# Retention steps of 128 tokens split into two halves of 64, every product in a 64x64 quarter of the matmul array

## The chip, the cores and the metric

One core of a Trainium2 chip runs the whole program. The metric is the device time of one execution in microseconds (us), as the median of three runs. The engines that matter here are TensorE (PE in the profile, its weight loads PEld), VectorE (DVE), ScalarE (ACT), GpSimd (POOL, used here for one scaling and a few transfers) and SyncE (SP, whose queue issues nearly all the DMAs).

## What is computed

A retention layer (linear attention with a decay for each head) is followed by two pairs of dense layers. The retention, cut to what matters:

```
gamma = 1 - 2 ** (-5 - arange(H))
for t in range(S):
    state = gamma * state + k[t] outer v[t]          # for each batch and head, 64 x 64
    y[t]  = scale * q[t] @ state
```

with 4 batches, 8 heads, 768 tokens and head size 64. Its output, 3072 tokens of 512 channels, goes through `x @ w_in`, `h - tanh(h)`, `@ w_out` (512 to 2048 to 512) and then through a second such pair with an ELU between. Weights come as 64-bit arrays and are converted in the kernel; the dense products are made as three fp32r products each of high and low parts.

## The kernel before

Tokens are taken in six blocks of 512: 128 tokens of each of the four batches. A retention step `s` (0 to 23 in the code, so the change's steps 5 to 24 are `s` = 4 to 23) treats one batch's 128 tokens of one block, and the four steps of block b run while the first dense layer works on block b - 1. `s // 4` is the block, `s % 4` the batch. Steps 0 to 3 have functions of their own (`scores0`, `out0`, `state0`), since no state comes before them.

A step has two places in TensorE's order. `ret_scores` puts eight fp32 matmuls there (`scores_mm`, L350: contraction over the 64 rows of a head, 128 keys by 128 queries), then VectorE multiplies both halves by the decay mask `dtab` into `pt` (L315) and scales q in place by `qtab` (L357). One dense group pair later `ret_out` puts `out_mm` there: eight matmuls of state by q (L374, 64 rows, 64 columns, 128 queries), eight of `pt` by v (L380, 128 rows, 64 columns, 128 queries), and `state_mm`, eight of k by v (L388, 128 rows, 64 columns, 64 wide). After it ScalarE and VectorE write the high and low part of the result to the dense layer's input `x` (L306, L309), and VectorE multiplies the state by gamma to the 128th (L584) and adds the new part (L312). In the last block (`s` = 20 to 23) no state is made.

An fp32 matmul leaves two records of MATMUL and two of LDWEIGHTS in the trace, so eight matmuls stand as sixteen.

The dense first layer takes 12 matmuls of 512 columns for a slice of `h` (`first_std`) and 12 for the four `acc` tiles (`second`), all at L410, alternating through the order list `order0`; `events` says after which `h` group a step's scores and its out come. Loads for a step are requested two or three groups ahead (`loads`). A planner (`Plan`) fixes, before the program runs, the order on every engine and the place of every tile from estimated durations and due times; tiles of class A (4 KB a partition) share 37 places, of class B 16, PSUM has 8. TensorE's own order is the one in which the code calls `op("PE", ...)`, and each engine runs its order strictly.

During the first quarter of steps (`s` = 4 to 7) the weights of the first layer are still being loaded and converted, by ScalarE (L326, L306) and VectorE (L330, L334, L309).

Of the kernel before, what the change touches and what calls it, by code (L numbers as in the profile page):

```python
# [264 lines left out]
def retention_moe_kernel(ctx: ExitStack, tc: tile.TileContext, dims, ins, out):  # L265
# [10 lines left out]
    NQ = NF // 2  # L276
    assert H * D == DM and 2 * D == P and B == SPB and NB == NCH and S % P == 0 and NB % 2 == 0
# [6 lines left out]
    qtab = const.tile([P, NP, P], F32, name="qtab")  # L284
    dtab = const.tile([P, 2, NP, P], F32, name="dtab")
    ktab = const.tile([P, H, 1], F32, name="ktab")
    gtab = const.tile([P, NP, 1], F32, name="gtab")
# [56 lines left out]
    def half(p, j):  # L344
        j = (j + p) % 2
        return slice(j * D, (j + 1) * D)

    def scores_mm(sc, qk):
# [6 lines left out]
    def scale_q_(qk):  # L355
        q = qk[:, 0, :].rearrange("p (a i) -> p a i", a=NP)
        nc.vector.tensor_tensor(out=q, in0=q, in1=qtab, op=ALU.mult)  # L357

    def scale_k_(kn):
        k = kn.rearrange("p (h d) -> p h d", h=H)  # L360
        nc.gpsimd.tensor_tensor(out=k, in0=k, in1=ktab.to_broadcast([P, H, D]), op=ALU.mult)

    def out_first_mm(o, v, pt):
        for p, j, r in pairs():
            h = 2 * p + j
            nc.tensor.matmul(
                out=o[half(p, j), p, :], lhsT=v[:, h * D:(h + 1) * D], rhs=pt[:, j, p, :],
                start=True, stop=True, skip_group_check=True,
            )

    def out_mm(even, odd, stc, qk, v, pt):
        outs = [(even, odd)[p % 2][:, p // 2, :] for p in range(NP)]
        for p, j, r in pairs():
            nc.tensor.matmul(  # L374
                out=outs[p][half(p, j)], lhsT=stc[r, p, :], rhs=qk[r, 0, p * P:(p + 1) * P],
                start=(p < 2), stop=False, skip_group_check=True,
            )
        for p, j, r in pairs():
            h = 2 * p + j
            nc.tensor.matmul(  # L380
                out=outs[p][half(p, j)], lhsT=v[:, h * D:(h + 1) * D], rhs=pt[:, j, p, :],
                start=False, stop=True, skip_group_check=True,
            )

    def state_mm(ds, v, kn):
# [7 lines left out]
    def state_view(odd):  # L393
        return odd[:, NP // 2:, :].rearrange("p a (b d) -> p (a b) d", d=D)

    def load_qk(t, s):
        nc.sync.dma_start(out=t, in_=ins["qkv"][s][:, 0:2, :])

# [16 lines left out]
    with tc.manual_schedule():  # L415
# [15 lines left out]
        nc.scalar.dma_start(out=dtab, in_=ins["dtab"])  # L431
        nc.scalar.dma_start(out=ktab, in_=ins["ktab"])
        nc.scalar.dma_start(out=gtab, in_=ins["gtab"])
# [3 lines left out]
        taken = {"m0", "b4"}  # L437
# [3 lines left out]
            {"raw": 12, "g": 4, "gl": 8, "qk": 2, "pt": 1, "pt0": 2, "w1r": 5, "T": 1, "wop": 4, "w2r": 8, "r3": 1,  # L441
             "v": 4, "kn": 4, "w32": 4, "ev": 4, "raw2": 2, "r": 5},
# [11 lines left out]
        QK, V, KN, PT, ST = {}, {}, {}, {}, {}  # L454
# [82 lines left out]
        def ret_load(s, rel):  # L537
            if s not in QK:
                t = QK[s] = Buf("A", [P, 2, TB], F32, f"qk{s}", "qk")
                dma(lambda: load_qk(t.ap, s), 4096, w=[t], rel=rel)  # L540
            if s not in V:
                t2 = V[s] = Buf("B", [P, TB], F32, f"v{s}", "v")
                dma(lambda: load_v(t2.ap, s), 2048, w=[t2], rel=rel)
            if s // B == NCH - 1:
                return
            if s not in KN:
                t3 = KN[s] = Buf("B", [P, TB], F32, f"kn{s}", "kn")
                dma(lambda: load_kn(t3.ap, s), 2048, w=[t3], rel=rel)
            k = KN[s]
            op("POOL", 1.2, lambda: scale_k_(k.ap), w=[k], name=f"scalek{s}")  # L550

        def ret_scores(s):
            q = QK[s]
            c = [Buf("P", [P, NP, P], F32, f"sc{s}_{j}") for j in range(2)]
            op("PE", 1.55, lambda: scores_mm([x.ap for x in c], q.ap), r=[q], w=c, lat=0.2, name=f"scores{s}")
            p = PT[s] = Buf("A", [P, 2, NP, P], F32, f"pt{s}", "pt")
            for j in range(2):
                op("DVE", DVE5, lambda j=j: mul(p.ap[:, j], c[j].ap, dtab[:, j]), r=[c[j]], w=[(p, j)], name=f"mask{s}")
            op("DVE", DVE5, lambda: scale_q_(q.ap), r=[qtab_b], w=[q], name=f"scaleq{s}")

        def ret_out(s):
            b, c = divmod(s, B)
            q, vv, p, sv = QK.pop(s), V.pop(s), PT.pop(s), ST[c // 2]
            even = Buf("P", [P, NP // 2, P], F32, f"oe{s}")
            odd = Buf("P", [P, NP, P], F32, f"oo{s}")
            op("PE", 1.8, lambda: out_mm(even.ap, odd.ap, sv.ap[:, c % 2], q.ap, vv.ap, p.ap),
               r=[q, vv, p, (sv, c % 2)], w=[even, (odd, 0)], lat=0.2, name=f"out{s}")
            last = b == NCH - 1
            if not last:
                k = KN.pop(s)  # L570
                op("PE", 0.6, lambda: state_mm(state_view(odd.ap), vv.ap, k.ap), r=[k, vv], w=[(odd, 1)], lat=0.2, name=f"state{s}")
            if c == 0:
                x_tile(b)
            x = X[b]
            sl = slice(c * P, (c + 1) * P)
            for i, (ks, o) in enumerate(((slice(0, NP, 2), even), (slice(1, NP, 2), odd))):
                def view(o=o, i=i):
                    return o.ap if i == 0 else o.ap[:, 0:NP // 2, :]

                op("ACT", 0.32, lambda ks=ks, view=view: copy(x.ap[:, 0, ks, sl], view()), r=[o], w=[(x, (0, c, i))], due=3.0, name=f"xhi{s}")  # L580
                op("DVE", 0.36, lambda ks=ks, view=view: sub(x.ap[:, 1, ks, sl], view(), x.ap[:, 0, ks, sl].bitcast(F32)),
                   r=[o, (x, (0, c, i))], w=[(x, (1, c, i))], due=4.0, name=f"xlo{s}")
            if not last:
# [144 lines left out]
        qtab_b = Buf("D")  # L728
# [7 lines left out]

        def load0_kn(s):
            t = KN[s] = Buf("B", [P, TB], F32, f"kn{s}", "kn")
            dma(lambda: load_kn(t.ap, s), 2048, w=[t], name=f"kn{s}")
            op("POOL", 1.2, lambda: scale_k_(t.ap), w=[t], name=f"scalek{s}")  # L740

        def scores0(s):
            c = [Buf("P", [P, NP, P], F32, f"sc{s}_{j}") for j in range(2)]
            op("PE", 1.15, lambda: scores_mm([x.ap for x in c], stage.ap[:, s]), r=[(stage, s)], w=c, lat=0.2, name=f"scores{s}")
            p = PT[s] = Buf("A", [P, 2, NP, P], F32, f"pt{s}", "pt0")
            for j in range(2):
                op("DVE", DVE5, lambda j=j: mul(p.ap[:, j], c[j].ap, dtab[:, j]), r=[c[j]], w=[(p, j)], name=f"mask{s}")
# [13 lines left out]
        def state0(j):  # L761
            ds = Buf("P", [P, 2, NP, D], F32, f"dsp{j}")
            for c in range(2):
                vv, k = V.pop(2 * j + c), KN.pop(2 * j + c)
                op("PE", 0.7, lambda c=c, vv=vv, k=k: state_mm(ds.ap[:, c], vv.ap, k.ap), r=[vv, k], w=[(ds, c)], lat=0.2, name=f"state{2 * j + c}")
            t = ST[j] = Buf("B", [P, 2, NP, D], F32, f"st{j}")
            op("ACT", ACT5, lambda: copy(t.ap, ds.ap), r=[ds], w=[t], name=f"st{j}")
# [3 lines left out]
        dma(lambda: nc.sync.dma_start(out=qtab, in_=ins["qtab"]), 2048, w=[qtab_b], due=FAR, name="qtab")  # L771
        for s in range(B):
            load0_kn(s)
        scores0(0)
# [45 lines left out]
        for b, f, lo, hi in order0:  # L820
            h = first_std(W[0, f], X[b], n)
            for what, s in events.get(n, []):
                {"scores": ret_scores, "out": ret_out, "state0": state0}[what](s)
            y = tanhshrink(h, n)
# [251 lines left out]
```

## Time and profile before

| | |
|---|---|
| median of three runs | 1083.55 us (1083.25 to 1084.83) |
| the profiled execution | 1084.41 us |
| its span, first to last instruction | 1082.3 us |
| PE busy | 1072.2 us (99%) |
| DVE busy | 897.4 us (83%) |
| ACT busy | 713.2 us (66%) |
| chain that ended last | PE 93%, DVE 5% |
| DMA moved | 239.85 MB, mean 222 GB/s |

Busy time of PE counts overlapping matmuls once; whether PE is really full is read from the distance between starts of matmuls, not from the busy share. The span is what a sum over the profile is made against; some 2 us of the execution lie outside it.

### The profile page before, as it was taken

To read this page: it belongs to the slowest core of one execution; us is meant where nothing else is said; L and a number is where in the kernel's file an instruction comes from. 1 tells how busy PE (TensorE), PEld (TensorE's weight loads), DVE (VectorE), ACT (ScalarE), POOL (GpSimd) and SP (SyncE) were. 2 spreads that over 40 slices of the span, in tenths; PEclk is the share of its full clock that TensorE was granted. 3 is DMA by queue.
4 is the path that set the end of the run, shared out by engine and by line. 5 is a ranking of instruction groups with operands and counts; after the bars stand their busy time and mean duration, and the time that the engine had idled before them with its cause. 6 is when DMAs were issued, how large, how long until landed. Compare 5 with 4: busy or idle time off the path is not lost.

```text
span 1082.3 us, 15911 instructions
## 1 busy us (share of the span) xinstructions
PE 1072.2 (99%) x5745; PEld 873.4 (81%) x5745; DVE 897.4 (83%) x1494; ACT 713.2 (66%) x1292; POOL 28.1 (3%) x28
## 2 busy tenths in 40 slices
PE   8999999999999999999999999999999999999998
PEld 5778888888888888788887888888888888888886
DVE  5997998678888888888899589987877978878965
ACT  3766885465666565666677599944689854789652
POOL 1100002000000000000000000000000000000000
PEclk9999999999999999999999999999999999999999
DMA  9736365527668666865598199047955149862353
GB/s 357 281 135 250 112 227 180 163 41 246 237 241 289 246 248 237 319 254 203 205 323 291 66 356 387 15 164 299 364 203 214 71 163 367 296 244 104 127 204 136
DMA packets 99229, 239.85 MB, mean 222 GB/s; under 512 B 7632, under 2 KB 42448, under 8 KB 96464
## 3 DMA queue, kind: packets, MB, share of 16 engines
q1 hardware_dynamic: 98144, 236.22, 60.1%
q0 software_dynamic: 576, 2.10, 1.1%
q8 instruction: 45, 0.74, 0.3%
q10 hardware_dynamic: 432, 0.53, 0.2%
q14 instruction: 32, 0.26, 0.1%
HBM read 186.39 MB, written 52.43 MB: 221 GB/s over the span
## 4 chain that ended last, share of the span: by engine, by line
PE 93%; DVE 5%; DMA 1%; issue 1%; ACT 0%; SPq 0%; DVEq 0%
PE acc L410 23%; PE h L410 22%; PE xo L410 12%; PE x L410 12%; PE zo L410 6%; PE z L410 6%; PE w L410 3%; PE wo L410 3%; PE sc L350 2%; PE oe L380 1%; PE oe L374 1%; PE oo L380 1%; DVE w L334 1%; DMA kn<-qkv 1%; PE oo L388 1%
## 5 line engine op out<-in xcount | busy, mean ns | idle before, releaser
L410 PE MATMUL acc<-g,w 128*128 128x512 f32 x1152 | 282.6, 394 | 0.6 <-DVE g L309 0.6
L410 PE MATMUL h<-x,w 128*128 128x512 f32 x1152 | 279.6, 391 | 2.5 <-ACT w L306 2.2
L410 PEld LDWEIGHTS h<-x,w 128*128 128x128 f32 x1152 | 216.8, 189 | 49.5 <-ACT w L306 2.8
L410 PEld LDWEIGHTS acc<-g,w 128*128 128x128 f32 x1152 | 213.1, 188 | 48.6 <-DVE g L309 1.4
L306 ACT ACTIVATE g<-y 128x512 fp32r<-128x512 f32 x240 | 141.4, 624 | 149.3 <-DVE y L623 121.1
L309 DVE TENSOR_TENSOR g<-y,g 128x512 fp32r<-128x512 f32 x240 | 161.7, 694 | 42.6 <-ACT g L306 42.3
L410 PE MATMUL xo<-g,w 128*128 128x512 f32 x576 | 133.6, 390 | 0.0
L410 PEld LDWEIGHTS xo<-g,w 128*128 128x128 f32 x576 | 107.7, 188 | 24.0 <-ACT ou L306 1.9
L410 PE MATMUL x<-xh,q 128*128 128x512 f32 x384 | 127.0, 389 | 0.0
L618 DVE SCALAR_TENSOR_TENSOR y<-y,u 128x512 f32<-128x512 f32 x96 | 66.6, 694 | 36.5 <-ACT y L612 33.8
L410 PEld LDWEIGHTS x<-xh,q 128*128 128x128 f32 x384 | 72.1, 188 | 15.0
L612 ACT ACTIVATE u<-h 128x512 f32<-128x512 f32 x96 | 57.0, 594 | 39.8 <-PE h L410 37.5
L641 DVE SCALAR_TENSOR_TENSOR y<-y,t 128x512 f32<-128x512 f32 x96 | 65.6, 685 | 14.9 <-ACT t L636 14.6
L623 DVE COPY_PREDICATED y<-m,h 128x512 f32<-128x512 uint16 x96 | 70.7, 736 | 5.2 <-ACT m L612 1.1
L410 PE MATMUL x<-xl,q 128*128 128x512 f32 x192 | 74.7, 389 | 0.0
L612 ACT ACTIVATE m<-u,xs_b 128x512 bf16<-128x512 f32 x96 | 69.6, 725 | 0.0
L612 ACT ACTIVATE y<-u,qa_b 128x512 f32<-128x512 f32 x96 | 69.3, 722 | 0.0
L620 DVE SCALAR_TENSOR_TENSOR y<-y,h 128x512 f32<-128x512 f32 x96 | 65.5, 683 | 1.8
L410 PE MATMUL z<-xh,q 128*128 128x512 f32 x192 | 66.9, 389 | 0.0
L309 DVE TENSOR_TENSOR h<-h,t 128x512 f32<-128x512 f32 x96 | 66.4, 691 | 0.0
L410 PE MATMUL zo<-g,w 128*128 128x512 f32 x288 | 66.3, 389 | 0.0
L410 PEld LDWEIGHTS zo<-g,w 128*128 128x128 f32 x288 | 54.1, 188 | 11.2
(101 smaller groups left out, 1427.9 us busy)
## 6 DMA issues: line engine op xcount, KB each, us to landing
w<-w3d SPq DMA_DIRECT2D x21, 2048.0 KB, 8.4
q<-w2d SPq DMA_DIRECT2D x72, 512.0 KB, 6.4
raw<-w SPq DMA_DIRECT2D x64, 512.0 KB, 6.9
w<-w1d SPq DMA_DIRECT2D x64, 512.0 KB, 7.2
qk<-qkv SPq DMA_DIRECT2D x20, 512.0 KB, 5.4
w1d<-w SPq DMA_DIRECT2D x16, 512.0 KB, 2.8
v<-qkv SPq DMA_DIRECT2D x24, 256.0 KB, 6.0
x1d<-o SPq DMA_DIRECT2D x12, 512.0 KB, 3.5
```

Of the source, the lines that this page charges most:

```text
L306: nc.scalar.activation(out=out_, in_=in_, func=AF.Copy)
L309: nc.vector.tensor_tensor(out=out_, in0=a, in1=b, op=ALU.subtract)
L334: nc.vector.scalar_tensor_tensor(out=wu, in0=raw.bitcast(U32)[:, 0::2], scalar=29, in1=wu, op0=ALU.logical_shift_right, op1=ALU.bitwise_or,)
L350: nc.tensor.matmul(out=sc[j][:, p, :], lhsT=qk[r, 1, p * P:(p + 1) * P], rhs=qk[r, 0, p * P:(p + 1) * P], start=True, stop=True,)
L374: nc.tensor.matmul(out=outs[p][half(p, j)], lhsT=stc[r, p, :], rhs=qk[r, 0, p * P:(p + 1) * P], start=(p < 2), stop=False, skip_group_chec ...
L380: nc.tensor.matmul(out=outs[p][half(p, j)], lhsT=v[:, h * D:(h + 1) * D], rhs=pt[:, j, p, :], start=False, stop=True, skip_group_check=True,)
L410: nc.tensor.matmul(out=out_, lhsT=lhs(a), rhs=rhs(b), skip_group_check=True, start=(first and at == 0 and i == 0), stop=(last and at == n ...
L612: op("ACT", dur, lambda: nc.scalar.activation(out=o.ap, in_=i.ap, func=func, **kw), r=r, w=w, name=f"{func}{name}")
L618: op("DVE", DVE5, lambda: nc.vector.scalar_tensor_tensor(out=y.ap, in0=y.ap, scalar=QB, in1=u.ap, op0=ALU.add, op1=ALU.mult), r=[u], w=[y])
L620: op("DVE", DVE5, lambda: nc.vector.scalar_tensor_tensor(out=y.ap, in0=y.ap, scalar=C2, in1=h.ap, op0=ALU.mult, op1=ALU.mult), r=[h], w=[y ...
L623: op("DVE", 0.65, lambda: nc.vector.copy_predicated(out=y.ap, mask=m.ap.bitcast(U16), data=h.ap), r=[m, h], w=[y], due=9.0)
L641: op("DVE", DVE5, lambda: nc.vector.scalar_tensor_tensor(out=yv(), in0=yv(), scalar=1.0, in1=t.ap, op0=ALU.add, op1=ALU.mult), r=[t], w=[k])
```

## The change

Each step's 128 tokens are split into two halves `c` of 64. Scores are made only inside a half, so sixteen matmuls of 64 by 64 by 64 replace eight of 64 by 128 by 128. The state is brought up to date after each half, by sixteen matmuls with 64 rows of tokens (eight in the last block, where only the first half's is needed); it now stands in the same two PSUM banks as the scores and is made at the scores' place in TensorE's order, with k and v then. The outputs are sixteen matmuls of state by q and sixteen of `pt` by v, all of 64 by 64 by 64. Consecutive matmuls go to the four different quarters of the array.

The state is kept without decay: k is scaled by gamma to the power of (384 - t) and q by gamma to the power of (t - 384), with t the token's place in the whole sequence, so `qtab` is loaded anew for each block and `ktab` holds all blocks; the multiplication of the state by gamma (L584) is gone. q is loaded a second time, in another order, together with v (`qv`, 512 KB a step) and scaled there; the masks become one table of half the width (the first block's old mask table is kept in a class A place for that time); `pt` moves from class A to class B, and class A has 36 places; states move to class C.

```diff
-    A_TAGS = [f"a{i}" for i in range(32)] + ["qa", "qb", "pt", "ga", "gb"]
+    A_TAGS = [f"a{i}" for i in range(32)] + ["qa", "qb", "ga", "gb"]
-    C_TAGS = ["m0", "m1"]
+    C_TAGS = [f"m{i}" for i in range(9)]
...
+    def scores_mm(sc, qk):
+        for p in range(NP):
+            for c, t in halves():
+                for j in range(2):
+                    at = slice((j * NP + p) * HP, (j * NP + p + 1) * HP)
+                    nc.tensor.matmul(
+                        out=sc[c][j * HP:(j + 1) * HP, 0, p, :], lhsT=qk[t, 1, at], rhs=qk[t, 0, at],
+                        start=True, stop=True, skip_group_check=True,
+                    )
...
+    def out_mm(o, st, qv, pt):
+        for c, t in halves():
+            for p, j, r in pairs():
+                at = slice((c * NP + p) * HP, (c * NP + p + 1) * HP)
+                nc.tensor.matmul(
+                    out=o[j][half(p), p // 2, t], lhsT=st[c][r, p, :], rhs=qv[r, 0, at],
+                    start=(p < 2 and c == 0), stop=False, skip_group_check=True,
+                )
+        for c, t in halves():
+            for p, j, r in pairs():
+                at = slice((c * NP + p) * HP, (c * NP + p + 1) * HP)
+                nc.tensor.matmul(
+                    out=o[j][half(p), p // 2, t], lhsT=qv[r, 1, at], rhs=pt[r, c, p, :],
+                    start=False, stop=True, skip_group_check=True,
+                )
...
+    def state_mm(ds, v, kn, n):
+        for p in range(NP):
+            for c, t in halves()[:n]:
+                for j in range(2):
+                    h = 2 * p + j
+                    nc.tensor.matmul(
+                        out=ds[c][j * D:(j + 1) * D, 1, p, :], lhsT=kn[t, h * D:(h + 1) * D],
+                        rhs=v[t, h * D:(h + 1) * D], start=True, stop=True, skip_group_check=True,
+                    )
...
             if s not in QK:
                 t = QK[s] = Buf("A", [P, 2, TB], F32, f"qk{s}", "qk")
                 dma(lambda: load_qk(t.ap, s), 4096, w=[t], rel=rel)
+            t4 = QV[s] = Buf("A", [P, 2, TB], F32, f"qv{s}", "qv")
+            dma(lambda: load_qv(t4.ap, s), 4096, w=[t4], rel=rel, due=30.0)
...
-            if s // B == NCH - 1:
-                return
...
         def ret_scores(s):
+            b, i = divmod(s, B)
+            q, vv, k, qv = QK.pop(s), V.pop(s), KN.pop(s), QV[s]
+            n = 1 if b == NCH - 1 else 2
+            sc = [Buf("P", [P, 2, NP, HP], F32, f"sc{s}_{c}") for c in range(2)]
+            op("PE", 0.9, lambda: scores_mm([x.ap for x in sc], q.ap), r=[q], w=[(x, 0) for x in sc], lat=0.2, name=f"scores{s}")
+            op("PE", 0.2 + 0.2 * n, lambda: state_mm([x.ap for x in sc], vv.ap, k.ap, n), r=[k, vv],
+               w=[(x, 1) for x in sc[:n]], lat=0.2, name=f"state{s}")
+            p = PT[s] = Buf("B", [P, 2, NP, HP], F32, f"pt{s}", "pt")
+            st = [ST[i]]
+            for c in range(2):
+                op("DVE", 0.36, lambda c=c: mul(p.ap[:, c], sc[c].ap[:, 0], dtab), r=[sc[c], dtab_b], w=[(p, c)], due=6.0, name=f"mask{s}")
+            for c in range(n):
+                t = Buf("C", [P, NP, D], F32, f"st{s}_{c}")
+                op("DVE", 0.36, lambda c=c, t=t, f=st[c]: add(t.ap, sc[c].ap[:, 1], f.ap), r=[sc[c], st[c]], w=[t], due=6.0, name=f"sta{s}")
+                st.append(t)
+            S01[s] = st[:2]
+            ST[i] = st[-1]
+            op("DVE", DVE5, lambda: scale_q_(qv.ap), r=[qtab_b], w=[(qv, 0)], name=f"scaleq{s}")
...
         def ret_out(s):
+            o = [Buf("P", [P, NP // 2, P], F32, f"o{s}_{j}") for j in range(2)]
+            op("PE", 1.25, lambda: out_mm([x.ap for x in o], [x.ap for x in st], qv.ap, p.ap),
+               r=[qv, p, *st], w=o, lat=0.2, name=f"out{s}")
-                op("DVE", 0.36, lambda: nc.vector.tensor_tensor(
-                    out=sv.ap[:, c % 2], in0=sv.ap[:, c % 2], in1=gtab.to_broadcast([P, NP, D]), op=ALU.mult),
-                   w=[(sv, c % 2)], due=4.0, name=f"stg{s}")
-                op("DVE", 0.36, lambda: add(sv.ap[:, c % 2], state_view(odd.ap), sv.ap[:, c % 2]),
-                   r=[odd], w=[(sv, c % 2)], due=4.0, name=f"sta{s}")
```

## Rows read from the trace of the kernel before

**Rows 1.** Busy time of engines by stretch of the span, all engines.

```profile
core 0: us, PE busy (x) PEld busy (x) DVE busy (x) ACT busy (x) POOL busy (x), PEclk, DMA share, GB/s
...
24.00:75.00 51.00, 49.27 (x449) 38.96 (x450) 49.59 (x92) 37.91 (x70) 5.13 (x4) 1.00 0.65 233
...
430.00:535.00 105.00, 105.00 (x601) 84.83 (x600) 87.37 (x154) 65.90 (x122) 0.00 (x0) 1.00 0.69 253
```

**Rows 2.** The same for a shorter stretch, columns as in rows 1.

```profile
48.00:64.00 16.00, 15.85 (x116) 11.89 (x114) 16.00 (x30) 11.36 (x22) 1.06 (x1) 1.00 0.69 240
```

**Rows 3.** Timeline of PE, scores of step 17: start us, us, instruction.

```profile
332.71 0.84 PE L410 MATMUL h<-x,w 128*128 128x512 f32 x3
333.48 1.16 PE L350 MATMUL sc<-qk 64*128 64x128 f32 x16
334.58 0.50 PE L410 MATMUL acc<-g,w 128*128 128x512 f32 x1
```

**Rows 4.** Timeline of PE, out and state of step 17.

```profile
339.70 0.61 PE L410 MATMUL h<-x,w 128*128 128x512 f32 x2
340.24 0.33 PE L374 MATMUL oe<-qk,st 64*64 64x128 f32 x2
...
340.40 0.28 PE L374 MATMUL oe<-qk,st 64*64 64x128 f32 x2
340.42 0.28 PE L374 MATMUL oo<-qk,st 64*64 64x128 f32 x2
340.51 0.28 PE L374 MATMUL oe<-qk,st 64*64 64x128 f32 x2
...
341.77 0.63 PE L388 MATMUL oo<-v,kn 128*64 128x64 f32 x16
342.33 0.72 PE L410 MATMUL acc<-g,w 128*128 128x512 f32 x2
```

**Rows 5.** Timeline of PE's weight loads, first eight of the same block.

```profile
340.24 0.14 PEld L374 LDWEIGHTS oe<-qk,st 64*64 64x64 f32 x2 [0.35 <-issue]
...
340.30 0.14 PEld L374 LDWEIGHTS oe<-qk,st 64*64 64x64 f32 x2
```

**Rows 6.** Timeline of PE, out of step 24, in the last block.

```profile
516.11 0.61 PE L410 MATMUL h<-x,w 128*128 128x512 f32 x2
...
518.27 0.50 PE L410 MATMUL acc<-g,w 128*128 128x512 f32 x1
```

**Rows 7.** Tile oo's instructions: durations in ns, least, median, most; first and last start.

```profile
L388 PE MATMUL oo<-v,kn x256: 219/222/223, 33.0 to 418.4; 128*64 128x64 f32 x128
```

**Rows 8.** Groups of DVE instructions by shape: busy us, mean ns, then idle before.

```profile
L315 DVE TENSOR_TENSOR pt<-sc,dtab 128x512 f32<-128x512 f32 x48 | 31.1, 683 | 14.8 <-PE sc L350 14.8
...
L357 DVE TENSOR_TENSOR qk<-qk,qtab 128x512 f32<-128x512 f32 x20 | 14.1, 705 | 0.0
...
L584 DVE TENSOR_TENSOR st<-st,gtab 128x256 f32<-128x256 f32 x16 | 6.7, 418 | 0.0
L312 DVE TENSOR_TENSOR st<-oo,st 128x256 f32<-128x256 f32 x16 | 6.7, 417 | 1.7 <-ACT x L306 1.7
```

**Rows 9.** Timeline of PE, step 5, with idle time and its releaser.

```profile
27.07 3.01 PE L410 MATMUL h<-x,w 128*128 128x512 f32 x12
31.47 0.33 PE L374 MATMUL oe<-qk,st 64*64 64x128 f32 x2 [1.38 <-DVE qk L357]
```

**Rows 10.** Timeline of POOL: scaling of k, steps 5 and 6, then step 17.

```profile
28.73 2.04 POOL L361 TENSOR_TENSOR kn<-kn,ktab 128x512 f32<-128x512 f32 x2 [7.87 <-DMA kn<-qkv]
...
326.03 1.04 POOL L361 TENSOR_TENSOR kn<-kn,ktab 128x512 f32<-128x512 f32 x1 [24.23 <-DMA kn<-qkv]
```

**Rows 11.** Tile w1d: the queue's loads, duration ns, first and last issue.

```profile
L492 SPq DMA_DIRECT2D w<-w1d x64: 319/449/1664, 198.8 to 582.0; - x64
```

**Rows 12.** Tile acc: matmuls that use those loads, first and last start.

```profile
L410 PE MATMUL acc<-g,w x1152: 387/389/502, 37.6 to 622.7; 128*128 128x512 f32 x192
```

More of the change, by code (lines that the diff above doesn't have):

```diff
@@ L282, in retention_moe_kernel @@
     dram = ctx.enter_context(tc.tile_pool(name="dram", bufs=1, space=bass.MemoryType.DRAM))
[L284 to L287, printed above, removed]
+    qtab = const.tile([P, TB], F32, name="qtab")
+    dtab = const.tile([P, NP, HP], F32, name="dtab")
+    ktab = const.tile([P, NCH, H, 1], F32, name="ktab")
     qa_b = const.tile([P, 1], F32, name="qa_b")
@@ L342, in pairs, with half, halves, first_scores_mm @@
         return [(p, j, slice(j * D, (j + 1) * D)) for p in range(NP) for j in range(2)]
[L344 to L348, printed above, removed]
+    def half(p):
+        return slice((p % 2) * D, (p % 2 + 1) * D)
+    def halves():
+        return [(c, slice(c * HP, (c + 1) * HP)) for c in range(2)]
+    def first_scores_mm(sc, qk):
         for p, j, r in pairs():
@@ L360, in scale_k_, with scale_q_ @@
+    def scale_q_(qv):
+        nc.vector.tensor_tensor(out=qv[:, 0, :], in0=qv[:, 0, :], in1=qtab, op=ALU.mult)
+    def scale_k_(kn, b):
         k = kn.rearrange("p (h d) -> p h d", h=H)
-        nc.gpsimd.tensor_tensor(out=k, in0=k, in1=ktab.to_broadcast([P, H, D]), op=ALU.mult)
+        nc.gpsimd.tensor_tensor(out=k, in0=k, in1=ktab[:, b].to_broadcast([P, H, D]), op=ALU.mult)
     def out_first_mm(o, v, pt):
-        for p, j, r in pairs():
+        for p, j in [(a + i, j) for a in range(0, NP, 2) for j in range(2) for i in range(2)]:
@@ L365, in out_first_mm @@
             h = 2 * p + j
             nc.tensor.matmul(
-                out=o[half(p, j), p, :], lhsT=v[:, h * D:(h + 1) * D], rhs=pt[:, j, p, :],
+                out=o[half(p), j * NP // 2 + p // 2, :], lhsT=v[:, h * D:(h + 1) * D], rhs=pt[:, j, p, :],
                 start=True, stop=True, skip_group_check=True,
             )
[L371 to L383, printed above, removed]
@@ L430, in retention_moe_kernel @@
                 jobs0 += [(0, hi), (0, hi + 1)]
-        nc.scalar.dma_start(out=dtab, in_=ins["dtab"])
+        dt0 = place("A", "a31", [P, 2, NP, P], F32, "dtab0")
+        nc.scalar.dma_start(out=dt0, in_=ins["dtab"])
         nc.scalar.dma_start(out=ktab, in_=ins["ktab"])
-        nc.scalar.dma_start(out=gtab, in_=ins["gtab"])
-        taken = {"m0", "b4"}
+        taken = {"m0", "b4", "a31"}
         slots = {"A": A_TAGS, "B": B_TAGS, "C": C_TAGS, "X": X_TAGS, "P": P_TAGS}
@@ L549, in ret_load @@
             k = KN[s]
-            op("POOL", 1.2, lambda: scale_k_(k.ap), w=[k], name=f"scalek{s}")
+            op("POOL", 1.2, lambda: scale_k_(k.ap, s // B), w=[k], name=f"scalek{s}")
         def ret_scores(s):
[L553 to L558, printed above, removed]
@@ L559, in ret_scores @@
-            op("DVE", DVE5, lambda: scale_q_(q.ap), r=[qtab_b], w=[q], name=f"scaleq{s}")
-        def ret_out(s):
[L562 to L572, printed above, removed]
+            b, i = divmod(s, B)
@@ L574, in ret_out @@
             x = X[b]
[L575 to L582, printed above, removed]
@@ L583, in ret_out @@
-            if not last:
-                op("DVE", 0.36, lambda: nc.vector.tensor_tensor(
-                    out=sv.ap[:, c % 2], in0=sv.ap[:, c % 2], in1=gtab.to_broadcast([P, NP, D]), op=ALU.mult),
-                   w=[(sv, c % 2)], due=4.0, name=f"stg{s}")
-                op("DVE", 0.36, lambda: add(sv.ap[:, c % 2], state_view(odd.ap), sv.ap[:, c % 2]),
-                   r=[odd], w=[(sv, c % 2)], due=4.0, name=f"sta{s}")
+            sl = slice(i * P, (i + 1) * P)
+            for j in range(2):
+                ks = slice(j * NP // 2, (j + 1) * NP // 2)
+                op("ACT", 0.32, lambda ks=ks, o=o[j]: copy(x.ap[:, 0, ks, sl], o.ap), r=[o[j]], w=[(x, (0, i, j))], due=3.0, name=f"xhi{s}")
+                op("DVE", 0.36, lambda ks=ks, o=o[j]: sub(x.ap[:, 1, ks, sl], o.ap, x.ap[:, 0, ks, sl].bitcast(F32)),
+                   r=[o[j], (x, (0, i, j))], w=[(x, (1, i, j))], due=4.0, name=f"xlo{s}")
@@ L735, in load0, with load_qtab @@
             dma(lambda: load_v(t.ap, s), 2048, w=[t], name=f"v{s}")
+        def load_qtab(b, rel):
+            dma(lambda: nc.sync.dma_start(out=qtab, in_=ins["qtab"][b - 1]), 2048, w=[qtab_b], rel=rel, due=FAR, name=f"qtab{b}")
         def load0_kn(s):
@@ L764, in state0 @@
                 vv, k = V.pop(2 * j + c), KN.pop(2 * j + c)
-                op("PE", 0.7, lambda c=c, vv=vv, k=k: state_mm(ds.ap[:, c], vv.ap, k.ap), r=[vv, k], w=[(ds, c)], lat=0.2, name=f"state{2 * j + c}")
-            t = ST[j] = Buf("B", [P, 2, NP, D], F32, f"st{j}")
-            op("ACT", ACT5, lambda: copy(t.ap, ds.ap), r=[ds], w=[t], name=f"st{j}")
+                op("PE", 0.7, lambda c=c, vv=vv, k=k: first_state_mm(ds.ap[:, c], vv.ap, k.ap), r=[vv, k], w=[(ds, c)], lat=0.2, name=f"state{2 * j + c}")
+            for c in range(2):
+                t = ST[2 * j + c] = Buf("C", [P, NP, D], F32, f"st{2 * j + c}")
+                op("ACT", 0.32, lambda c=c, t=t: copy(t.ap, ds.ap[:, c]), r=[ds], w=[t], name=f"st{2 * j + c}")
         for s in range(B):
             load0(s)
-        dma(lambda: nc.sync.dma_start(out=qtab, in_=ins["qtab"]), 2048, w=[qtab_b], due=FAR, name="qtab")
         for s in range(B):
             load0_kn(s)
+        dma(lambda: nc.sync.dma_start(out=dtab, in_=ins["dtab_half"]), 1024, w=[dtab_b], due=FAR, name="dtab")
+        load_qtab(1, 0)
         scores0(0)
@@ L823, in retention_moe_kernel @@
                 {"scores": ret_scores, "out": ret_out, "state0": state0}[what](s)
+                if what == "scores" and s % B == B - 1 and s // B < NCH - 1:
+                    load_qtab(s // B + 1, now_pe())
             y = tanhshrink(h, n)
```

59 lines of the change are left out of this document (37 added, 22 removed).

## The prediction

> **What bounds the kernel now.** I read the page first, then busy time by stretch, then TensorE's timeline around single retention steps, because a busy share says nothing about how full TensorE is. Across the last block's stretch PE is busy for 105.00 of 105.00 us and VectorE for 87.37 [rows 1]. What counts is the distance between starts: twelve dense matmuls, the last of them 0.39 us long, take 3.01 us where nothing came before, and in steady state one starts every 0.23 us (0.61 less 0.39 is 0.22 for the pair in front of a step) [rows 4, 9, 12]. TensorE's order is fixed, and in the middle of the kernel the view of waits shows none in front of a retention block, only the entry to it. So a block's cost is the distance from the start of the last dense matmul before it to the first one after it, and time taken from such a block comes off the end, as long as what it needs is there.
>
> The exception is the stretch while the first weights are converted: there VectorE is busy for 49.59 of 51.00 us, and 16.00 of 16.00 between 48 and 64 us [rows 1, 2]. There VectorE sets the pace, and TensorE's small stalls are its echo, such as the 1.38 us in front of step 5's out, which waits for the scaled q [rows 9].
>
> **TensorE's blocks before.** Scores: the last `h` matmul starts at 332.71 + 0.84 - 0.39 = 333.16, the first `acc` at 334.58, so 1.42 us [rows 3]. Out and state: from 339.70 + 0.61 - 0.39 = 339.92 to 342.33, 2.41 us [rows 4]. In the last block, where no state is made: from 516.33 to 518.27, 1.94 us [rows 6]. A step is 3.83 us, in the last block 3.36.
>
> **What a block of quarters costs.** The rows give each piece.
> - Entry: 339.92 to 340.24, 0.32 us. The first group of four records starts there, the second at 340.40; the 0.16 between is one weight load (0.05: the second set of loads starts at 340.30, 0.06 after the first at 340.24) and one stream of 128 columns (0.11, from 340.40 to 340.51) [rows 4, 5]. With 64 columns the stream halves, so 0.11 from first to second.
> - The beat. Four records, two of `oe` and two of `oo`, start at 340.40 and 340.42 and the next ones at 340.51: four quarters work side by side, at 0.109 us for four [rows 4]. No row shows four quarters with 64 columns. The nearest is L388: 64 columns, two halves of the array at a time, sixteen records in 0.63 us with the last 0.22 long, so (0.63 - 0.22) / 7 = 0.0586 us a pair [rows 4, 7]. That pair loads the whole array with weights and streams 64 columns through all of it, which is just what four quarters do. The bounds are therefore 0.053 (half of L374's beat, rounded down a little) and 0.109 (halving the columns gains nothing). I take 0.0586, by the row that moves the same data in the same time.
> - Exit: L388's last pair starts at 342.18, the dense matmul at 342.33, 0.15 us; and 0.02 inside the last group [rows 4].
>
> A block of sixteen groups (64 records by four) is then 0.32 + 0.11 + 14 x 0.0586 + 0.02 + 0.15 = 1.42 us. Scores and state together are such a block, where scores alone took 1.42; out is another, where out and state took 2.41. In the last block the eight state matmuls use one half of the rows, so they go two at a time, and eight groups of two take as long as eight of four: 1.42 again. Saved: 2.41 - 1.42 = 0.99 us a step, in the last block 1.94 - 1.42 = 0.52.
>
> **VectorE.** A step loses two masks of 0.683, the multiplication by gamma of 0.418 and one addition of 0.417, 2.20 us; it gains two masks and two additions of half the width, by the 0.417 of that shape 1.67 us. So 0.53 less; the scaling of q (0.705) stays, but no longer has to wait for the scores [rows 8].
>
> **Other queues.** SP gets 512 KB more a step and POOL four more scalings of 1.04 us [rows 10]; DMA is at 0.65 to 0.69 of its time in these stretches and POOL nearly idle [rows 1], so I price both at nothing, with the cover named: k is now wanted at the scores. For step 17 its scaling ends at 327.07 and the scores begin at 333.48, 6.4 us of cover [rows 3, 10]. `qtab`'s reload has the four dense group pairs between blocks. A place of class A less, and two more wanted, could delay weight loads; the last `w1d` load is issued at 582.0 and the last matmul that uses one starts at 622.7, so loads run far ahead, and I price that at nothing too [rows 11, 12].
>
> **The first four steps** are paid where VectorE rules. Steps 5 to 7 give what VectorE gives, 3 x 0.53 = 1.6 us; step 8 falls behind the last stall and gives TensorE's 0.99. Together 2.6. The bounds: nothing (a new wait eats it) and 4 x 0.99 + 1.38 = 5.3 (VectorE catches up and the wait for the scaled q vanishes too).
>
> **The sum.** Steps 9 to 20: 12 x 0.99 = 11.9. Steps 21 to 24: 4 x 0.52 = 2.1. First four: 2.6. Together 16.6 us. The profiled execution, 1084.41 us, would take 1067.8; its time stands 0.86 above the median, so the median goes from 1083.55 to 1067.0.
>
> A rule against the change: the Trainium skill, TensorE: Matmul & The Clock Gate, section "Wait — 56ns, not 53.3ns?", says that starts of matmuls never come closer than about 25 ns, however few columns they have. By that a group of four takes 0.100 us and not 0.0586; an estimate from the page, with the terms of the first rival below, is some 8 us slower than before. The trace disagrees within a group (starts at 340.40 and 340.42 for four records), but on average it nowhere shows a record in less than 0.027 [rows 4], so the rule is not refuted for the whole block.
>
> **The rivals.**
> - A floor on records. If 0.109 us for four is not the stream of 128 columns but what four records cost, a block of sixteen groups is 0.32 + 16 x 0.109 + 0.02 + 0.15 = 2.23, a step 4.46 against 3.83, 0.63 more; last block: 0.32 + 8 x 0.109 + 8 x 0.0586 + 0.17 = 1.83 and 2.23, 0.70 more. 16 x 0.63 + 4 x 0.70 = 12.9 us slower, 1096.4. It decides from a beat of 0.089, where two blocks cost what a step costs now. For: no row is denser. Against: the four starts lie within 0.02, and the beat of 0.109 is twice that of L388 at twice its columns. 7 in 100.
> - Quarters taken two at a time, if order or banks let only pairs through: thirty-two pairs at 0.0586 are 0.54 + 31 x 0.0586 = 2.36 a block; a step 4.72, 0.89 more, and much the same in the last block: 17 to 18 us slower, 1101. Against it: L374 already runs four with both row halves writing to one bank; here each has its own. 4 in 100.
> - The state waits for k in step 5. Its place is now right behind step 5's scores, before 27.07; k's scaling for steps 5 and 6 runs from 28.73 to 30.77, the first half ending at 29.75 [rows 9, 10]. If the load isn't moved forward as far, TensorE stands for up to 2.7 us, and the first four steps give nothing: 16.6 - 2.7 = 13.9, so 1069.7. For: the queue is crowded there, with a q and v load more. Against: the order of loads follows need, and VectorE, which rules there, goes on with weights meanwhile. 15 in 100.
> - The forecast itself: 73 in 100. It has its own range, 1063 to 1070: the first four steps between 0 and 5.3, the beat between 0.053 and 0.062 (3 us one way, 2 the other). One in 100 is left for no change.
>
> **Range and chances.** 1062.5 to 1071.5 holds the forecast with its bounds and the third rival, and leaves out the two slower ones and the tails. Within 0.2% (2.2 us) this kernel's runs can't be told from no change. Faster 0.88, same 0.02, slower 0.10.
>
> **What would show it.** Groups of four records every 0.055 to 0.062 us on the scores', state's and out's lines; both blocks of a step near 1.42 from dense start to dense start; no idle in front of the out blocks after 75 us; two masks of about 0.42 and no gamma multiplication on VectorE. The prediction is wrong if the beat is above 0.07, if TensorE waits for k, v, q or the state sum at a step, or if the dense part after 520 us becomes longer.

## The result and the profile after

The changed kernel takes 1067.12 us (median of four, 1066.64 to 1068.86) against 1083.4 us (four runs of the kernel before, 1083.14 to 1084.83): ratio 0.985, 95% interval 0.9833 to 0.9867, 16.3 us less. The forecast was 1067.0, with 16.6 us less. The profiled execution took 1066.64 us, its span is 1064.9 against 1082.3 us.

TensorE's timeline for step 17, the scores block and the out block, and for the last scores block (step 24); columns as in [rows 3, 4 and 6]:

```profile
321.62 0.61 PE L435 MATMUL h<-x,w 128*128 128x512 f32 x2
322.17 0.70 PE L363 MATMUL sc<-qk 64*64 64x64 f32 x32
322.68 0.65 PE L413 MATMUL sc<-v,kn 64*64 64x64 f32 x32
323.26 0.50 PE L435 MATMUL acc<-g,w 128*128 128x512 f32 x1
...
328.38 0.61 PE L435 MATMUL h<-x,w 128*128 128x512 f32 x2
328.93 0.70 PE L388 MATMUL o<-qv,st 64*64 64x64 f32 x32
329.44 0.65 PE L395 MATMUL o<-pt,qv 64*64 64x64 f32 x32
330.02 0.50 PE L435 MATMUL acc<-g,w 128*128 128x512 f32 x1
...
492.38 0.61 PE L435 MATMUL h<-x,w 128*128 128x512 f32 x2
492.93 0.69 PE L363 MATMUL sc<-qk 64*64 64x64 f32 x32
493.44 0.63 PE L413 MATMUL sc<-v,kn 64*64 64x64 f32 x16
494.01 0.50 PE L435 MATMUL acc<-g,w 128*128 128x512 f32 x1
```

The last `h` matmul starts at 321.62 + 0.61 - 0.39 = 321.84 and the first `acc` at 323.26: 1.42 us for scores and state, where scores alone took 1.42 [rows 3]. The out block goes from 328.60 to 330.02, 1.42 us again, where out and state took 2.41 [rows 4]. The last product's 32 records take 0.65 us with the last 0.22 long; by eight groups of four that is (0.65 - 0.22 - 0.02) / 7 = 0.0586 us a group. Read from single starts, the blocks are 1.409 to 1.410 us from step 6 on, the scores blocks of the last four steps 1.396, and groups start every 0.058.

VectorE's groups of a step, columns as in [rows 8]:

```profile
L315 DVE TENSOR_TENSOR pt<-sc,dtab 128x256 f32<-128x256 f32 x40 | 15.0, 413 | 0.0
L312 DVE TENSOR_TENSOR st<-sc,st 128x256 f32<-128x256 f32 x36 | 14.9, 415 | 1.3 <-PE sc L413 1.0
L369 DVE TENSOR_TENSOR qv<-qv,qtab 128x512 f32<-128x512 f32 x20 | 13.7, 683 | 0.0
```

Two masks and two additions at 0.41 stand where masks of 0.683 and two state operations stood [rows 8].

Where the time came from, by distances between starts of dense matmuls in the two timelines (us):

| stretch | before | after | less | forecast |
|---|---|---|---|---|
| start to first dense matmul | 19.23 | 18.47 | 0.76 | 0 |
| from there to the last one before step 9's scores | 137.88 | 135.38 | 2.50 | 2.6 |
| from there to the last one before step 21's scores (12 steps) | 277.68 | 265.60 | 12.08 | 11.9 |
| from there to the first one after step 24's out (4 steps) | 83.48 | 81.32 | 2.16 | 2.1 |
| from there to the end | 564.03 | 564.11 | -0.08 | 0 |

The first steps are not like the others. TensorE's timeline there, and busy time by stretch, columns as in [rows 9 and 1]:

```profile
18.47 4.94 PE L435 MATMUL h<-x,w 128*128 128x512 f32 x12 [1.75 <-ACT w L306]
...
25.35 0.70 PE L363 MATMUL sc<-qk 64*64 64x64 f32 x32
25.87 0.65 PE L413 MATMUL sc<-v,kn 64*64 64x64 f32 x32
26.45 3.01 PE L435 MATMUL h<-x,w 128*128 128x512 f32 x12
29.39 0.70 PE L388 MATMUL o<-qv,st 64*64 64x64 f32 x32
29.90 0.41 PE L395 MATMUL o<-pt,qv 64*64 64x64 f32 x15
30.90 0.47 PE L395 MATMUL o<-pt,qv 64*64 64x64 f32 x17 [0.59 <-issue]
```

```profile
24.00:75.00 51.00, 49.22 (x718) 37.64 (x714) 49.83 (x99) 39.49 (x77) 3.44 (x3) 1.00 0.78 294
36.00:48.00 12.00, 10.92 (x103) 7.66 (x102) 12.00 (x25) 10.05 (x20) 1.28 (x1) 1.00 0.98 377
48.00:64.00 16.00, 16.00 (x193) 12.23 (x196) 16.00 (x32) 11.46 (x22) 1.04 (x1) 1.00 0.76 269
```

Step 5's state follows its scores without a gap, so the wait for k did not come; nor does the 1.38 us wait for the scaled q [rows 9]. TensorE stands instead for 0.59 us in the middle of step 5's out, where the profile names no releaser; that block takes 2.22 us. VectorE is as full as before (16.00 of 16.00 between 48 and 64 us, as in [rows 2]), and DMA is at 0.98 of its time between 36 and 48 us, where the kernel before had 0.86.

Of the five stretches, the two from step 9 to step 24 are firm: 265.60 and 81.32 us stand to the hundredth in every experiment below that leaves TensorE's blocks alone. The first two stretches are not: the experiments show below that both move by 1 us and more from one execution to the next of the same order of work.

### The profile page after: what moved, and what is told of

Its sections match the earlier page's. It is cut to its first block, busy times and chain, and to the rows that moved or that the text cites. A ratio compares the mean times of both kernels' runs of the same rounds, so it can differ in the third digit from the quotient of the medians.

```text
span 1064.9 us, 18550 instructions
## 1 busy us (share of the span) xinstructions
PE 1055.2 (99%) x7025; PEld 859.8 (81%) x7025; DVE 891.3 (84%) x1498; ACT 712.2 (67%) x1294; POOL 32.6 (3%) x32
## 4 chain that ended last, share of the span: by engine, by line
PE 92%; DVE 5%; DMA 1%; issue 1%; ACT 1%; SPq 0%; DVEq 0%; ACTq 0%
PE acc L435 23%; PE h L435 22%; PE xo L435 12%; PE x L435 12%; PE z L435 6%; PE zo L435 6%; PE w L435 3%; PE wo L435 3%; PE o L388 1%; PE sc L363 1%; PE o L395 1%; PE sc L413 1%; DVE w L334 1%; DMA qv<-qv 1%; DVE y L644 1%
## 5 line engine op out<-in xcount | busy, mean ns | idle before, releaser
L309 DVE TENSOR_TENSOR g<-y,g 128x512 fp32r<-128x512 f32 x240 | 162.6, 698 | 41.9 <-ACT g L306 41.0
L665 DVE SCALAR_TENSOR_TENSOR y<-y,t 128x512 f32<-128x512 f32 x96 | 65.6, 685 | 14.9 <-ACT t L660 14.6
L309 DVE TENSOR_TENSOR h<-h,t 128x512 f32<-128x512 f32 x96 | 66.4, 691 | 0.0
```

Source lines behind the costliest of these rows:

```text
L309: nc.vector.tensor_tensor(out=out_, in0=a, in1=b, op=ALU.subtract)
L665: op("DVE", DVE5, lambda: nc.vector.scalar_tensor_tensor(out=yv(), in0=yv(), scalar=1.0, in1=t.ap, op0=ALU.add, op1=ALU.mult), r=[t], w=[k])
```

## The experiments

Each edit is made in the changed kernel. Distances are those of the table above. The scaling on GpSimd has four runs, every other experiment one.

**Which matmuls run side by side.** The loops are turned so that consecutive matmuls stay in one half of the rows (the last line twice, in both products of out):

```diff
 def scores_mm(sc, qk):
-    for p in range(NP):
-        for c, t in halves():
+    for c, t in halves():
+        for p in range(NP):
...
 def state_mm(ds, v, kn, n):
-    for p in range(NP):
-        for c, t in halves()[:n]:
+    for c, t in halves()[:n]:
+        for p in range(NP):
...
 def out_mm(o, st, qv, pt):
-            for p, j, r in pairs():
+            for p, j, r in sorted(pairs(), key=lambda x: x[1]):
```

> The loops of the three products are reordered so that consecutive matmuls stay in one half of the rows and alternate between the two halves of the columns; the matmuls themselves, and the order on every other engine, are those of the changed kernel. Theory (four quarters side by side are the gain): only pairs run together at 0.058 us a pair, so a block of 64 records takes 0.6 + 30 x 0.058 = 2.35 us instead of 1.41, a step 1.9 us more, the last four steps 1.4 more, and the kernel is 30 to 36 us slower than the changed one, near 1100 us, slower than the kernel before. Rival (half the columns alone give the gain, whatever runs side by side): the beat of a pair falls to about 0.03 us, blocks stay near 1.41 and the time near 1067.

It took 1074.06 us: neither. The timeline of TensorE at step 9's scores:

```profile
154.02 0.84 PE L435 MATMUL h<-x,w 128*128 128x512 f32 x3
154.79 0.80 PE L363 MATMUL sc<-qk 64*64 64x64 f32 x26
155.38 0.27 PE L413 MATMUL sc<-v,kn 64*64 64x64 f32 x2
155.43 0.28 PE L363 MATMUL sc<-qk 64*64 64x64 f32 x3
...
155.55 0.80 PE L413 MATMUL sc<-v,kn 64*64 64x64 f32 x27
156.28 0.50 PE L435 MATMUL acc<-g,w 128*128 128x512 f32 x1
```

State records of the first row half start at 155.38, ahead of the last scores of the second half at 155.43 and later: TensorE does not hold a free row half back for an earlier matmul that waits in the other one. So the block became 1.81 us, not 2.35; the out block, where the row half changes after four matmuls and not eight, only 1.46. Turned this way, the order costs 0.40 us a scores block and 0.05 an out block, far less than I had priced it. But it did not force pairs, as it was meant to: for part of each block four quarters still ran side by side. What pairs alone cost is shown by the next experiment.

**What sets the beat.** Nine blocks of sixteen extra fp32 matmuls, of which nothing is read, stand behind dense groups without a retention step:

```diff
+    def probe_mm(b, rows, cols, m, n):
+        flat = dtab.rearrange("p a i -> p (a i)")
+        tiles = [(i, j) for i in range(rows) for j in range(cols)]
+        for k in range(16):
+            i, j = tiles[k % len(tiles)]
+            r = slice(i * HP, (i + 1) * HP)
+            nc.tensor.matmul(
+                out=b[i][j * HP:j * HP + m, 0:n], lhsT=flat[r, 0:m], rhs=flat[r, 0:n],
+                start=True, stop=True, skip_group_check=True,
+            )
...
```

> Nine blocks of sixteen extra fp32 matmuls (64 rows, with a mask table as both operands, into spare banks that nothing reads) stand behind dense groups without a retention step: four quarters with 128, 64, 32 and 16 streamed columns, pairs with 64 and 16, one quarter alone with 64 and 16, and four quarters with 32 weight columns and 64 streamed. Theory (the beat of 0.058 us is the loading of 64 weight columns, 0.053, plus a little): 0.058 at 64, 32 and 16 columns, whether four, two or one quarter is used, 0.109 at 128, and a little less, 0.053 to 0.056, with 32 weight columns. Rival A (streaming sets it): 0.03 at 32 and 0.015 to 0.02 at 16 columns. Rival B (each record costs 0.0146 us): 0.058 for four at 64 and below, 0.029 for a pair at 16 and 0.015 for one alone at 16.

TensorE's timeline, each line one block: four quarters with 128, 32, 16 columns, pairs with 64 and 16, one alone with 64 and 16, four with 64, four with 32 weight columns:

```profile
240.50 1.10 PE L424 MATMUL probe<-dtab 64*64 64x128 f32 x32
266.20 0.67 PE L424 MATMUL probe<-dtab 64*64 64x32 f32 x32
291.43 0.66 PE L424 MATMUL probe<-dtab 64*64 64x16 f32 x32
341.04 1.15 PE L424 MATMUL probe<-dtab 64*64 64x64 f32 x32
366.75 1.11 PE L424 MATMUL probe<-dtab 64*64 64x16 f32 x32
392.42 2.08 PE L424 MATMUL probe<-dtab 64*64 64x64 f32 x32
443.44 2.04 PE L424 MATMUL probe<-dtab 64*64 64x16 f32 x32
470.02 0.69 PE L424 MATMUL probe<-dtab 64*64 64x64 f32 x32
495.26 0.65 PE L424 MATMUL probe<-dtab 64*32 64x64 f32 x32
```

With these blocks the run takes 1080.50 us. With 64 weight columns and at most 64 streamed, thirty-two records take 0.66 to 0.69 us in four quarters, about 1.1 in two and 2.0 to 2.1 in one, and whether 64 or 16 columns are streamed changes that by 0.03 to 0.04. Between starts the distance is 0.058 for one record in a quarter in every one of these blocks but two: 0.109 with 128 columns, 0.056 with 32 weight columns. So at 64 streamed columns and below a quarter that loads 64 weight columns takes a record each 0.058 us, and a pair of quarters takes no more and no less than four. Both rivals fall: streaming (16 columns would be much faster) and a cost per record (a pair would be twice as fast as four).

That the weight load is what takes the 0.058 us, and not some fixed time for any record in a quarter, these blocks do not show by themselves: none has both few weight columns and few streamed ones, and in the one with 32 weight columns the 64 streamed ones may set the beat. The kernel before speaks for the load: with 128 columns streamed, its pairs start every 0.112 us where a record loads 128 weight columns (L350) and every 0.109 where it loads 64 (L380). The Trainium skill, TensorE: Matmul & The Clock Gate, section "Wait — 56ns, not 53.3ns?", gives about 25 ns as the least distance between starts; here records of different quarters start 7 ns apart and average 14.6 ns over a group, so that floor does not hold across quarters.

**TensorE's share.** The score matmuls are made twice:

```diff
-        for p in range(NP):
+        for p in [*range(NP), *range(NP)]:
```

> The sixteen score matmuls of each of steps 5 to 24 are made twice, the second time over the same results. Theory: eight more groups of four at 0.058 us, 0.47 us more in each scores block; steps 8 to 24 pay all of it (17 x 0.47 = 7.9 us), steps 5 to 7 pay little or nothing because VectorE sets the pace there; 1075 to 1076.5 us. Rival (TensorE sets the pace in steps 5 to 7 too): 20 x 0.47 = 9.3 us, and the distance from the first dense matmul to step 9's scores grows by 1.9 us.

1075.79 us, 8.7 more than the changed kernel. The scores block is 1.877 us, 0.467 more; steps 9 to 20 take 271.20 instead of 265.60, 12 x 0.467 exactly. From the first dense matmul to step 9 it is 136.90, 1.52 more: step 8's 0.47 and another 1.05, more than the theory gave to steps 5 to 7. TensorE's timeline of step 6 shows what lay there:

```profile
34.70 1.16 PE L363 MATMUL sc<-qk 64*64 64x64 f32 x64
35.69 0.22 PE L413 MATMUL sc<-v,kn 64*64 64x64 f32 x1
36.86 0.69 PE L413 MATMUL sc<-v,kn 64*64 64x64 f32 x31 [0.95 <-issue]
```

0.95 us without a releaser, as in step 5's out above. So this run does not tell whether added TensorE time is free there, and a difference of 1 us in this stretch is within what single executions show, as the runs with added VectorE work bring out below.

**The price of changing the division of the array.** One matmul over all 128 rows stands between scores and state:

```diff
     def state_mm(ds, v, kn, n):
+        nc.tensor.matmul(
+            out=ds[0][0:D, 1, 0, :], lhsT=kn[:, 0:D], rhs=v[:, 0:D], start=True, stop=True, skip_group_check=True,
+        )
```

> One extra fp32 matmul of 128 rows by 64 columns stands between the scores and the state of each step, in a place that the state then overwrites, so each scores block changes the array's division twice more. Theory (each change costs about 0.16 us, as between the two products of out in the kernel before: 0.11 more to the first record and 0.05 more to the second group): the scores block grows from 1.41 by 0.35 to 0.45 us, the kernel by 6 to 9, 1073 to 1076 us. Rival (a change costs nothing of its own): the block grows by the matmul's two beats alone, 0.12 us, and the kernel by 2.4 us.

1074.61 us. The timeline of TensorE at step 9's scores:

```profile
155.77 0.69 PE L363 MATMUL sc<-qk 64*64 64x64 f32 x32
156.39 0.33 PE L409 MATMUL sc<-v,kn 128*64 128x64 f32 x2
156.65 0.69 PE L416 MATMUL sc<-v,kn 64*64 64x64 f32 x32
```

The block became 1.826 us, 0.417 more; without the matmul's own two beats of 0.058 that is 0.15 a change. The Trainium skill, TensorEngine Tiling (Array Packing), section "Key Properties", says that a change of tiling mode drains TensorE; a cost at every change agrees with that. Steps 9 to 20 took 270.56, 4.96 more (12 x 0.413), but from the first dense matmul to step 9 only 0.53, and step 8 alone accounts for 0.42 of them: of the 1.25 us added to TensorE in steps 5 to 7 no more than 0.1 can be seen, in a stretch that differs by more between executions.

**VectorE's share.** Two multiplications that nothing reads are added to steps 5 to 8, and in another kernel to steps 9 to 20 (`if 2 * B <= s < 5 * B`):

```diff
                 st.append(t)
+                if s < 2 * B:
+                    for z in range(1):
+                        scr = Buf("C", [P, NP, D], F32, f"scr{s}_{c}_{z}")
+                        op("DVE", 0.36, lambda t=t, scr=scr: mul(scr.ap, t.ap, dtab), r=[t, dtab_b], w=[scr], due=6.0, name=f"extra{s}")
```

> Two extra VectorE multiplications of 128x256 (0.41 us each, into a tile that nothing reads) stand in each of steps 5 to 8, beside the state additions; 3.3 us of VectorE in all, 2.5 of them before step 8. Theory (VectorE sets the pace while the first weights are converted): the distance from the first dense matmul to step 9's scores grows from 135.4 by 1.6 to 3.3 us, the rest keeps its length; 1068.7 to 1070.4 us. Rival (VectorE is full there but not late): the distance grows by less than 0.6 us.

> The same two extra multiplications in each of steps 9 to 20, 9.9 us of VectorE in all. Theory (outside the first stretch TensorE sets the pace alone): no retention block and no dense group there becomes longer, the distance from step 9's scores to step 21's stays at 265.6 us, time 1067 within 1 us. Rival (VectorE is near its limit there as well): the distance grows by 2 us or more.

Early: 1070.89 us, and 138.47 from the first dense matmul to step 9, 3.09 more; the rest unchanged (265.60, 81.32). Late: 1068.76 us, and steps 9 to 20 at 265.60, unchanged to the last digit, with 24 operations more on VectorE. The time is outside the 1 us that was expected, but the difference lies ahead of what was added: the first dense matmul came at 19.50, 1.03 later, and step 9 another 1.04 later. All engines' busy time in the late kernel, then in the changed kernel in the same stretch, columns as in [rows 1]:

```profile
155.00:421.00 266.00, 266.00 (x2571) 216.78 (x2570) 230.53 (x430) 162.27 (x302) 22.42 (x16) 1.00 0.74 251
```
```profile
155.00:421.00 266.00, 266.00 (x2577) 216.84 (x2569) 226.18 (x406) 162.74 (x304) 18.04 (x16) 1.00 0.73 252
```

Three times the work costs nothing behind step 9. What it costs ahead of step 9 has to be read against single executions. Three other kernels give every engine the changed kernel's order up to step 9: this late one, the one with the probes, and the last experiment's. VectorE has the same 97 operations there between the first dense matmul and the end of step 8's out; their durations, added up, and the distance to step 9:

| run | VectorE, sum of durations | first dense matmul to step 9 |
|---|---|---|
| changed kernel | 58.05 | 135.38 |
| order of loads (last experiment) | 58.08 | 135.51 |
| late VectorE work | 59.44 | 136.42 |
| probes | 60.23 | 137.23 |
| early VectorE work (105 operations) | 61.93 | 138.47 |
| kernel before (96 operations) | 60.60 | 137.88 |

(Durations overlap a little, so that the sum exceeds the stretch.) The distance follows VectorE's sum, as it should where VectorE sets the pace, and the same order of work moves it by 1.85 us between executions. The kernels with pairs and with the extra matmul fit within 0.4 us; scores made twice (58.92 and 136.90) and q scaled on GpSimd (58.16 and 136.16, below) lie 0.8 and 0.6 us above what their sums would give, so the doubled scores seem to have been paid in part. So the 3.3 us of early work cost between 1.2 and 3.1; they also changed the planner's order of the early loads and conversions, which this run does not separate.

**Taking work off VectorE.** The scaling of q moves to GpSimd:

```diff
-        nc.vector.tensor_tensor(out=qv[:, 0, :], in0=qv[:, 0, :], in1=qtab, op=ALU.mult)
+        nc.gpsimd.tensor_tensor(out=qv[:, 0, :], in0=qv[:, 0, :], in1=qtab, op=ALU.mult)
...
-            op("DVE", DVE5, lambda: scale_q_(qv.ap), r=[qtab_b], w=[(qv, 0)], name=f"scaleq{s}")
+            op("POOL", 1.2, lambda: scale_q_(qv.ap), r=[qtab_b], w=[(qv, 0)], name=f"scaleq{s}")
```

> The scaling of q moves from VectorE (0.68 us a step) to GpSimd (about 1.05 us a step by its scaling of k). Theory (VectorE sets the pace while the first weights are converted, and nowhere else): steps 5 to 8 free 2.0 to 2.7 us of VectorE, and the distance from the first dense matmul to step 9's scores falls by 1.5 to 2.7 us from 135.4; from there to the end nothing changes; 1064.5 to 1065.6 us. Rival (the early stalls have another cause, loads or the fetching of instructions): that distance stays within 0.5 us, time 1067.

1069.23 us (four runs, 1067.82 to 1071.06), ratio to the kernel before 0.9866, interval 0.9846 to 0.9886: no gain over the changed kernel's 0.985. The distance to step 9 was 136.16, 0.8 more. The expected gain did not come. VectorE's other work became slower; its groups here, then in the changed kernel:

```profile
L334 DVE SCALAR_TENSOR_TENSOR w<-raw,w 128x512 uint32<-128x512 uint32 x64 | 46.7, 739 | 0.1
L330 DVE TENSOR_SCALAR w<-w 128x512 uint32<-128x512 uint32 x64 | 32.7, 518 | 1.8 <-ACT w L326 0.9
```
```profile
L334 DVE SCALAR_TENSOR_TENSOR w<-raw,w 128x512 uint32<-128x512 uint32 x64 | 44.4, 703 | 0.1
L330 DVE TENSOR_SCALAR w<-w 128x512 uint32<-128x512 uint32 x64 | 31.1, 494 | 2.1 <-ACT w L326 1.4
```

739 against 703 ns and 518 against 494, for the same operations. These means mix two kinds. In all ten traces an L330 that overlaps none of GpSimd's multiplications takes 400 to 434 ns and an L334 664 to 698 (both over 128x512); every slower one overlaps such a multiplication. The longest is in this run, one L330 in VectorE's timeline and what GpSimd's shows meanwhile:

```profile
231.65 3.12 DVE L330 TENSOR_SCALAR w<-w 128x512 uint32<-128x512 uint32 x1
231.86 1.39 POOL L373 TENSOR_TENSOR kn<-kn,ktab 128x512 f32<-128x512 f32 x1
232.87 1.61 POOL L369 TENSOR_TENSOR qv<-qv,qtab 128x512 f32<-128x512 f32 x1
```

In the stretch of the table above VectorE has five operations less here, 92, yet their durations add up to 58.16 us, as much as the changed kernel's 58.05: what it gave away came back as longer operations. The planner's order changed with it, and what that did by itself this run does not show.

**The first 0.76 us.** The program requests the first loads in the old order:

```diff
+        load_qtab(1, 0)
+        dma(lambda: nc.sync.dma_start(out=dtab, in_=ins["dtab_half"]), 1024, w=[dtab_b], due=FAR, name="dtab")
         for s in range(B):
             load0_kn(s)
-        dma(lambda: nc.sync.dma_start(out=dtab, in_=ins["dtab_half"]), 1024, w=[dtab_b], due=FAR, name="dtab")
-        load_qtab(1, 0)
```

> The loads of qtab and of the half mask table are requested ahead of the first four k tiles, as the kernel before had qtab; nothing else changes on any engine's order but the load queue. Theory: the first dense matmul came 0.76 us earlier in the changed kernel (18.47 against 19.23) because qtab no longer stood in front of loads that the first weights follow; with the order put back it comes at 18.9 to 19.4 and the kernel is 0.4 to 0.9 us slower. Rival (chance of one execution): it stays within 0.2 us of 18.47.

1068.02 us, the first dense matmul at 19.63. That would speak for the theory, but the edit did not do what it was meant to. The planner orders loads by when their data are due, and it left this queue as it was. The last of the first four k loads and qtab's, in this run and then in the changed kernel:

```profile
12.18 0.33 SPq L428 DMA_DIRECT2D kn<-qkv  x1
17.77 0.33 SPq L763 DMA_DIRECT2D qtab<-qtab  x1
```
```profile
12.54 0.33 SPq L428 DMA_DIRECT2D kn<-qkv  x1
17.82 0.43 SPq L763 DMA_DIRECT2D qtab<-qtab  x1
```

From the first instruction to the last, every engine and the load queue have the changed kernel's order. So this run is a second profiled execution of the changed kernel's work: the theory about qtab was not tested, but the same order brought the first dense matmul once at 18.47 and once at 19.63. The kernel before, at 19.23, lies between: nothing here shows the 0.76 us to be more than chance.

## Why the prediction was right

- The block of quarters: forecast 1.42 us, measured 1.41 in every step from the 6th on (1.40 for the scores blocks of the last four). The beat taken from L388, 0.0586, was the right row, because both load the same 64 weight columns a record; the prediction had argued by data moved, and the probes show that the streamed part of these data does not matter at 64 columns and below.
- Per step 0.99 forecast, 12.08 / 12 = 1.007 measured; in the last block 0.52 forecast, 2.16 / 4 = 0.54 measured. By records it comes from the scores and from `pt` by v, each now eight groups of 0.058 us where it was eight of 0.109 to 0.112, and from one change of the array's division less, at 0.15 us. State by q and k by v cost about what they did. These 16 steps make 14.2 of the 16.3 us, and in the changed kernel they repeat to the hundredth.
- The first four steps: forecast 2.6, measured 2.50. The reason held: the distance there follows VectorE's time, the 1.25 us that the extra matmul added to TensorE in steps 5 to 7 can hardly be seen, and of the 1.4 of the doubled scores some 0.8. That the size agrees to 0.1 is luck: the changed kernel's order took 135.38 to 137.23 us there in four executions, so against the one trace of the kernel before the gain is anything from 0.65 to 2.50.
- VectorE: forecast 0.53 less a step, so 8.5 us for sixteen steps and a little for the last four; its busy time fell by 6.1 (897.4 to 891.3). The step's own operations cost what was said (0.413 to 0.415 for 0.417). The conversion steps grew: L330 took 494 ns a time where the kernel before shows 28.0 us for its 64, or 444. In the changed kernel 14 of the 64 overlap a multiplication on GpSimd and average 762 ns, before it was 4; the others take 418 in both.
- DMA and GpSimd, priced at nothing: no wait for k came, and the part behind step 24 kept its length (564.03 and 564.11). But the cover was thinner than the argument had it. DMA stood at 0.98 between 36 and 48 us, and GpSimd, though nearly idle, makes the VectorE operations longer that it overlaps.
- The rivals. A cost per record and the wait for k did not occur. Nor did the second, quarters two at a time: groups of four start every 0.058 us. Its price was not tested by the whole kernel, since the experiment meant to force pairs (9.3 us faster than the kernel before) let the two row halves run past each other; the beat under it, 0.058 for a pair, is what the probes measured.
- The unforecast term is the 0.59 us in step 5's out. It is covered as far as these runs tell: in the kernels with pairs and with the extra matmul step 5's out took 1.48 and 1.51 us instead of 2.22, and the distance to step 9 was no shorter (135.87 and 135.91).
- The total: 16.6 forecast, 16.3 measured, with an interval of 14.4 to 18.1. The sum of the last 16 steps is right by its mechanism; the rest, some 2 us, agrees within what executions differ by.

## What to carry to other kernels

Cost a block of small matmuls from the start of the last large matmul before it to the first one after, and take the beat from the row that loads as many weight columns: on these runs a quarter that loads 64 took a record every 0.058 us with 64, 32 or 16 columns streamed, so halving the streamed columns below 64 gives nothing, while using all four quarters gives four times as much. Leaving out the masked half of a causal product pays only if the smaller products fill the array. Before pricing a saving at its engine's time, ask in each stretch which engine is late: 3.3 us of VectorE work cost 1.2 to 3.1 ahead of step 9, and three times as much cost nothing behind it. And before reading a difference of 1 us in such a stretch, look at how far executions of the same order differ there: 1.85 us here.

## What was not expected

- TensorE lets a row half run ahead of an earlier matmul that waits in the other half: records of the state started at 155.38 us ahead of scores that precede them in the program, starting at 155.43 and later. The strict order of an engine, as told of the kernel before, is the order in which it is given its work; between row halves starts can leave it.
- With dense blocks of small matmuls TensorE stood without a releaser in the profile, 0.59 us in step 5's out (changed kernel) and 0.95 us in step 6's scores (scores made twice), both while DMA was full (1.03 of its time between 24 and 36 us in either kernel). Later blocks of the same make, with DMA at about 0.75, show none. But full DMA alone does not bring it: with pairs and with the extra matmul DMA is at 1.03 there too, and TensorE is busy for 12.00 of these 12.00 us. Instructions that arrive late would explain it; it wasn't tried, and the cause stays open.
- A VectorE operation can take several times as long while GpSimd multiplies: an L330 takes 400 to 434 ns alone and up to 3.12 us beside GpSimd. How much it lengthens which one differs between executions of the same order: from the changed kernel to the one with probes three operations beside GpSimd in the early stretch (two L309, one L334) grew from 0.67 or 0.68 us each to between 1.23 and 1.53, 2.2 us together, as much as VectorE's sum grew.
